# Another beginning for a fused attention, expert and convolution kernel: unit 0 and the tails turned on TensorE, direct rows, new queue orders

## The chip, the cores and the metric

The kernel runs on one core of a Trainium2 chip. The metric is the device time of one execution in microseconds (us). All five engines take part: TensorE (PE) multiplies, VectorE (DVE), ScalarE (ACT) and GpSimd (POOL) work on tiles, and SyncE (SP) issues most of the transfers (DMAs); ACT and POOL issue some.

## The reference

Three layers follow each other; the change is in the first.

```
scores = q @ k.T / sqrt(D)                       # 4 x 8 heads, S = 576, D = 64, float32
cum    = cumsum(maximum(s, 0))
bias   = minimum(-(cum[:, None] - cum[None, :]), 0)
scores = where(causal, -1e9, scores + bias)
attn   = softmax(scores) @ v                     # -> x, [4, 576, 512]
x      = experts(x)      # 8 experts of 512 x 1024 x 512, one per token, relu, times its probability
h      = relu(x @ w_in); out = (h * sigmoid(conv3(h))) @ w_out
```

## The kernel before

float32 factors are kept as two float16 parts, "hi" and "lo", so that TensorE can multiply float16. The 32 heads are cut into 8 units of 4 heads. A unit's 576 rows are 512 main rows and 64 tail rows; the tails of all heads are prepared once.

Preparing unit u: `load` (L158) brings k and q into the buffers `st`; `split_hi` (ACT, L241) and `split_lo` (DVE L247 for units 0 and 1, POOL L249 and L250 after that) make the two parts; `turn` (L259) turns them with a DMA transpose on SP, two per unit, each for one half (e) of the rows; `copy` (DVE, L267) assembles 64 partitions of the tile `K1[u % 3]`. Rows 64 to 69 of that tile hold the running sum of s, in three float16 digits `cp` that `decay` makes for all heads. They go to DRAM (`ex`, `ext`; L593, L594, issued by ACT) and from there into the tile (`extra`, L263). Row 70 holds the row maxima.

Row maxima: `stage_a` (L334) multiplies hi by hi in up to 15 pieces per unit, DVE reduces each (L337); `max_turn` (PE, L400) and `max_out` (ACT, L405) make a row `mr`, which `max_row` (L412, L415) sends into row 70. Then `scores` (L432), exponentials on ACT (L471 to L477), the products with v (L504), normalization, and a store to `xd`. The v parts come by `loadv` (L168, L172; 12 transfers for one call) and `split_v`.

Order: a main loop of steps t. A unit has 14 steps, so unit u begins at step 14u, and step 0 is the first score product of unit 0. The table `PAR` says at which step, before its own beginning, a unit loads ('load', 'loadq' later for q), splits and turns ('at': k, q, turn half 0, turn half 1, extra), copies ('cp'), runs its pieces ('pa' over 'pn' steps) and makes its maxima ('mx'). The table 'start' orders the beginning. Each engine takes its instructions in the order in which the program emits them. SP's and ACT's transfers take eight semaphores in turn, and a transfer waits until the earlier transfer with its semaphore has landed.

The unit's chain at the beginning is: loads, splits, four transposes of unit 0 (halves apart), copies, rows from `ex`, six pieces for heads 0 and 1, `mr`, six pieces for heads 2 and 3, step 0. `turn_tail` (L277) turns the tails with four more transposes.

Of the kernel before, what the change touches and what calls it, by code (L numbers as in the profile page):

```python
# [9 lines left out]
F32 = mybir.dt.float32  # L10
F16 = mybir.dt.float16
# [31 lines left out]
class Keep:  # L43
# [6 lines left out]
PAR = {'u1': {'sv': -6, 'pa': -9, 'pn': 4, 'mx': -3},  # L50
 'u2': {'at': (-24, -23, -20, -20, -19), 'cp': (-18, -16), 'lv': -11, 'sv': -2, 'pa': -14, 'pn': 8, 'mx': -6},
 'u3': {'load': -37, 'loadq': 6, 'at': (-33, -28, -28, -27, -26.9), 'cp': (-23, -21), 'sv': -1, 'pa': -20, 'pn': 14, 'mx': -6},
 'u': {'load': -48,
       'loadq': 8,
       'at': (-38, -34, -28, -31, -26),
# [19 lines left out]
 'start': {'st': -4.88,  # L75
           'lk1': -3.883,
           'c1': -1.883,
           'pa': -1.88,
           'lq1': -0.877,
           'sk1': -0.843,  # L80
           'tt': -0.84,
           'lv0': -0.837,
           'sq1': -0.834,
           'lk2': -0.834,
           'mt0a': 0.129,
           'mo0a': 0.163,
           'mr0a': 0.166,
           'ct': 0.4,
           'pb': 0.377,
           'c2': 1.0,  # L90
           'pt': 1.003,
           'sv0': 1.103,
           'T10': 1.106,
           'mtt': 1.203,
           'mot': 1.3,
           'T11': 2.26,
           'x1': 2.269,
           'mtb': 2.297,
           'mob': 2.34,
           'mrt': 3.091,  # L100
           'lq2': 3.1,
           'mrb': 4.003,
           'z': 5.0,
           'lv1': 5.997},
# [8 lines left out]
def attention(tc, ctx, q, k, v, s, xd, rt, hook):  # L113
# [80 lines left out]
    for n in ("k", "q"):  # L194
        for b in range(B):
            G.dma_start(nt[32 * b:32 * b + 32, AT[n]], src[n][b, :, 512:576].rearrange("h (p t) d -> p h (t d)", t=2))
    constants(G, T1)
    make_identity(nc, ident)
    for t in (triq, trik, tailq):
        G.memset(t, 0.0)  # L200
    for e in range(2):
        r = slice(64 * e, 64 * e + 64)
        G.memset(tailk[r, e], 0.0)
        G.memset(tailk[r, 1 - e], -2.0 ** 15)
    for tq, tk, n in ((triq, trik, 64), (tailq, tailk, 32)):
# [63 lines left out]
    def split_tail(n):  # L269
        i = AT[n]  # L270
        a, h = nt[:, i].rearrange("p h (t d) -> p (h t) d", t=2), ht[:, i]
        A.activation(h[:, :, 1 - i], a, AF.Copy, scale=scale[n])
        V.scalar_tensor_tensor(h[:, :, i], in0=a, scalar=scale[n], in1=h[:, :, 1 - i], op0=ALU.mult, op1=ALU.subtract)

    def turn_tail():
        for b in range(B):
            Q.dma_start_transpose(out=T2[:, b].rearrange("d n (x p) -> d (n x) p", p=32), in_=ht[32 * b:32 * b + 32].rearrange("p n x y d -> p (n x y d)"))  # L277

    def copy_tail():
        for r, i in ((64, 0), (67, 1)):  # L280
            Q.dma_start(T1[r:r + 3, :, i], ext.rearrange("j (b h) c -> j b (h c)", b=B))
        for i in range(2):
            V.tensor_copy(T1[0:64, :, i], T2[64 - 64 * i:128 - 64 * i, :, i])
# [123 lines left out]
    def max_row(u, hs=slice(0, 4), tails=True):  # L407
        n = 0
# [173 lines left out]
    decay(0)  # L582
    split_hi(0, "k")
    split_lo(0, "k")
    decay(1)
    split_hi(0, "q")
    decay(2)
    split_lo(0, "q")
    for i in range(2):
        for e in range(2):  # L590
            turn(0, e, slice(i, i + 1))
    for e in range(2):
        A.dma_start(ex[:, e].rearrange("j r c -> r j c"), cp[:, :, 256 * e:256 * e + 256])  # L593
# [23 lines left out]
    def second_a():  # L617
        for f in P0[6:12]:
            f()()

    begin_tasks = dict(
        lk1=lambda: load(1, "k"), lq1=lambda: load(1, "q"), st=lambda: (split_tail("k"), split_tail("q")), tt=turn_tail, ct=copy_tail,
        lv0=lambda: loadv(0, 0, G), lv1=lambda: loadv(0, 1, G if PAR["h"]["vq"] else Q), c1=lambda: constants(G, K1[1]), c2=lambda: (constants(G, K1[2]), tctx.close()),
        pa=begin_a, sk1=lambda: split_qk(1, "k"), sq1=lambda: split_qk(1, "q"), mt0a=lambda: max_turn(0, first, False), mo0a=lambda: max_out(0, first, False),
        mr0a=lambda: max_row(0, first, False), T10=lambda: turn(1, 0), T11=lambda: turn(1, 1), x1=lambda: extra(1),
        pb=second_a, sv0=lambda: split_v(0), lk2=lambda: load(2, "k"), lq2=lambda: load(2, "q"),
        pt=lambda: [P0[12 + i]()() for i in range(3)], mtt=lambda: max_turn(0, None), mot=lambda: max_out(0, None), mrt=lambda: max_row(0, None),
        mtb=lambda: max_turn(0, second, False), mob=lambda: max_out(0, second, False), mrb=lambda: max_row(0, second, False),
        z=lambda: Q.dma_start(xd[NT:NT + 128].rearrange("p (j c) -> p j c", c=256), bc(zero[:, None, 0:256], [128, 4, 256])))
# [889 lines left out]
```

## Time and profile before

| | us |
|---|---|
| three runs | 718.02, 721.0, 721.49; median 721.0 |
| the profiled execution | 722.48, of which 720.8 from the first to the last instruction |
| attention | 0 to about 250 |
| routing and first experts | about 250 to 300 |
| experts | to about 490, then the third layer to 720.8 |

Over the span PE is busy 639.1 us (89%), DVE 446.1, ACT 385.8 and POOL 251.7. Some of the profile's views give busy time by stretch, with the granted clock of TensorE as a share of 2.4 GHz (0.50 is 1.2 GHz, the lower of its two levels). A timeline row begins with its start and its length; the bracket at its end is the idle time before it and what ended it. Rows with "q" behind the engine (SPq) are issues of transfers.

### The profile page before, as it was taken

The page shows a single profiled execution, that of the slowest core. Times are in us where ns is not written, and L with a number is a line of the kernel's source. Part 1 is how long each engine was busy: PE and PEld are TensorE (multiplying, and loading weights), DVE is VectorE, ACT ScalarE, POOL GpSimd, SP SyncE. Part 2 cuts the span into 40 slices and gives each one's busy share as a digit, 9 for nine tenths or more (in the row PEclk, how much of TensorE's full clock was granted, in tenths as well). Part 3 has the DMA queues.
Part 4 walks back from the last instruction along what each step waited for, and adds up shares of the span by engine and source line. Part 5 has one row for each costly group of instructions (what it writes and reads, how often), then busy time and mean ns, then how long its engine had stood idle before and what let it go on. Part 6 is the DMA issues. An engine that isn't in the chain of part 4 may idle for free. (4 is left out here: it accounts for less than half of the span.)

```text
span 720.8 us, 15276 instructions
## 1 busy us (share of the span) xinstructions
PE 639.1 (89%) x5087; PEld 399.5 (55%) x5087; DVE 446.1 (62%) x852; ACT 385.8 (54%) x650; POOL 251.7 (35%) x362
## 2 busy tenths in 40 slices
PE   0469699999999756899899899999889999999997
PEld 0247578887888633444444344444357766665443
DVE  5765578867976599563695868663129976455000
ACT  4142748785778656553653655532129965546010
POOL 9536766575144039932234544433100000000000
PEclk9985969997999859899999999999999999999999
DMA  9977474874568425899899996964184000000111
GB/s 183 183 148 138 68 163 107 159 138 84 128 206 272 126 69 185 248 335 239 200 311 257 272 280 194 259 128 104 48 149 101 16 15 16 30 30 16 58 45 58
DMA packets 175580, 103.89 MB, mean 144 GB/s; under 512 B 128150, under 2 KB 153534, under 8 KB 175486
## 3 DMA queue, kind: packets, MB, share of 16 engines
q1 hardware_dynamic: 170878, 89.70, 52.7%
q0 software_dynamic: 4272, 12.93, 5.9%
q8 instruction: 46, 0.75, 0.4%
q14 instruction: 48, 0.39, 0.2%
q10 hardware_dynamic: 336, 0.11, 0.1%
HBM read 62.20 MB, written 15.31 MB: 108 GB/s over the span
## 5 line engine op out<-in xcount | busy, mean ns | idle before, releaser
L1129 PE MATMUL hp<-r,xt 128*128 x504 | 114.1, 383 | 10.2 <-ACT xt L1160 7.1
L1129 PE MATMUL yp<-r,ht 128*128 x504 | 112.2, 379 | 1.7 <-PEq L1236 1.7
L1327 PE MATMUL hp<-yt,wi 128*128 128x288 f16 x768 | 97.1, 289 | 2.8 <-DMA yt<-yd 2.8
L1375 PE MATMUL o<-wo,g 128*128 128x512 f16 x432 | 94.5, 379 | 0.0
L1327 PEld LDWEIGHTS <-wi 128*128 128x128 f16 x768 | 75.8, 99 | 24.4 <-DMA yt<-yd 3.3
L1129 PEld LDWEIGHTS <-xt 128*128 128x128 f16 x504 | 49.8, 99 | 71.0 <-ACT xt L1160 9.6
L1129 PEld LDWEIGHTS <-ht 128*128 128x128 f16 x504 | 48.5, 98 | 57.4 <-issue 1.8
L1085 DVE SCALAR_TENSOR_TENSOR r<-st,r 128x512 f32 (+3 forms) x80 | 70.7, 950 | 6.2 <-ACT r L1074 4.5
L1074 ACT ACTIVATE r<-st 128x512 f32 (+3 forms) x84 | 57.1, 762 | 26.7 <-SPq L1122 22.1
L1375 PEld LDWEIGHTS <-g 128*128 128x128 f16 x432 | 42.3, 98 | 49.5
L337 DVE TENSOR_REDUCE mx<-za 128x1 f32<-128x384 f32 (+4 forms) x97 | 56.9, 602 | 17.4 <-PE za L334 16.7
L1190 POOL DMA_INDIRECT yd<-ys,idx x21 | 21.7, 1034 | 126.3 <-DVEq L1113 87.5
L476 ACT ACTIVATE phi<-z,lnes 128x512 f16<-128x512 f32 (+1 forms) x80 | 50.1, 627 | 29.3 <-PE z L435 29.2
L432 PE MATMUL z<-k 71*128 71x256 f16 (+2 forms) x320 | 55.4, 301 | 6.7 <-DMA k<-mr 4.2
L334 PE MATMUL za<-k 70*128 70x256 f16 (+2 forms) x160 | 37.4, 314 | 26.8 <-DMA k<-ex 20.8
L488 DVE TENSOR_TENSOR plo<-z,phi 128x512 f16<-128x512 f32 (+1 forms) x80 | 48.2, 603 | 12.1 <-ACT z L477 11.5
L1344 DVE SCALAR_TENSOR_TENSOR c<-hb,cw,c 128x576 f32<-128x576 f32 x32 | 26.1, 816 | 37.0 <-ACT c L1338 37.0
L504 PE MATMUL o<-v,p 128*128 128x65 f32 x256 | 48.1, 301 | 0.0
L477 ACT ACTIVATE z<-z,lnes 128x512 f32<-128x512 f32 (+1 forms) x80 | 47.9, 598 | 0.0
L1378 ACT ACTIVATE s<-o 128x512 f32<-128x512 f32 x18 | 10.7, 597 | 63.9 <-PE o L1375 63.9
L504 PE MATMUL o<-vv,phi 128*128 128x65 f16 (+1 forms) x512 | 43.7, 207 | 0.0
L504 PEld LDWEIGHTS <-phi 128*128 128x128 f16 x544 | 43.5, 112 | 0.0
(270 smaller groups left out, 1146.2 us busy)
## 6 DMA issues: line engine op xcount, KB each, us to landing
st<-in_moe_w_dram SPq DMA_DIRECT2D x8, 2048.0 KB
st<-in_moe_w_dram SPq DMA_DIRECT2D x24, 512.0 KB
out_dram<-s SPq DMA_DIRECT2D x18, 256.0 KB
st<-in_k_dram SPq DMA_DIRECT2D x16, 256.0 KB
st<-in_q_dram SPq DMA_DIRECT2D x16, 256.0 KB
xd<-xh SPq DMA_DIRECT2D x16, 256.0 KB
k<-in_moe_w_dram SPq DMA_DIRECT2D x8, 512.0 KB
s<-in_moe_w_in_dram SPq DMA_DIRECT2D x16, 256.0 KB
```

The source lines that it names most:

```text
L334: PE.matmul(out, lhsT=l, rhs=r, start=start, stop=stop, skip_group_check=True)
L337: return lambda: V.tensor_reduce(out, z.rearrange("p (e c) -> p e c", e=m), axis=AX.X, op=ALU.max)
L432: PE.matmul(out, lhsT=ks[i], rhs=qs[i], start=first and not i, stop=False, skip_group_check=True)
L476: A.activation(hi[:, 0:n], z[:, 0:n], AF.Exp, bias=lnes, scale=1.0 / SC)
L477: A.activation(p[:, 0:n], z[:, 0:n], AF.Exp, bias=lnes, scale=1.0 / SC)
L488: (V if md == "a" else G).tensor_tensor(lo[:, 0:n], p[:, 0:n], hi[:, 0:n], op=ALU.subtract)
L504: PE.matmul(out, lhsT=w, rhs=x, start=first, stop=last, skip_group_check=True)
L1074: i = self.nc.scalar.activation(hi, src, AF.Copy, scale=self.scale[w])
L1085: i = nc.vector.scalar_tensor_tensor(lo, in0=src, scalar=sc, in1=hi, op0=ALU.mult, op1=ALU.subtract)
L1129: i = self.nc.tensor.matmul(out, lhsT=lhsT, rhs=self.rings[w][:, c, k, bass.ds(s, 1), f], **kw)
L1327: PE.matmul(st[x][:, n, 0:HN], lhsT=wi[:, c, k, m], rhs=t[:, n, a + k], start=k + a + c == 0, stop=k == 3 and a == 4)
L1375: PE.matmul(o, lhsT=g[:, a, k, 128 * i:128 * i + 128], rhs=wo[:, c, k], start=j == 0, stop=j == 23)
```

## The change

- Unit 0 and the tails are turned on TensorE: `turned` multiplies four 128x128 blocks by an identity into a PSUM tile, and ACT or DVE copies it out in float16. Unit 0 has 8 such tiles, the tails 8. The eight DMA transposes at the beginning are gone.
- `extra_first`: unit 0's rows of `cp` go straight from on-chip memory into the tile, in 12 transfers on SP, instead of through `ex`. `ex` and `ext`, for the other units and the tails, are written by POOL.
- The tails are loaded by SP (k's ahead of the rows, q's after unit 1's loads) instead of POOL; the masks are made in another order; unit 0's maxima rows are issued by ACT.
- `busy`: idle products of 512 columns whose result nobody reads: 10 ahead of unit 0's turns, 4 ahead of the pieces, and 1 ahead of each of unit 0's 12 pieces.
- The pieces of heads 2 and 3, which were all emitted ahead of step 0's products, are spread over steps 1 to 4. Unit 1's pieces begin at step 7 instead of 5.
- Later units: q of unit 3 is loaded at step 6 instead of 11; units from 4 on load, split and turn 3 steps sooner, and half 1 is still turned ahead of half 0. q's lo part of unit 1 is made by POOL instead of DVE.

```diff
- 'u': {'load': -48,
+ 'u': {'load': -51,
        'loadq': 8,
-       'at': (-38, -34, -28, -31, -26),
+       'at': (-41, -37, -31, -34, -26),
...
+    def turned(h, i, j, out, copy):
+        z = zps.tile([128, 512], F32, name="z") if j % 2 else ops.tile([128, 512], F32, name="o")
+        for m in range(4):
+            PE.matmul(z[:, 128 * m:128 * m + 128], lhsT=h[:, i, 4 * j + m].rearrange("p y d -> p (y d)"), rhs=id16, start=m == 0, stop=m == 3, skip_group_check=True)
+        z = out(z, j)
+        if copy == "A":
+            A.activation(z[0], z[1], AF.Copy)
+        else:
+            V.tensor_copy(*z)
...
+    def extra_first(j):
+        for r, n in ((64, 0), (67, 1)):
+            for e in range(2):
+                Q.dma_start(K1[0][r + j:r + j + 1, e, n].rearrange("o (h c) -> o h c", h=NH), cp[0:NH, j, 256 * e:256 * e + 256])
...
+    def busy(z, n):
+        for _ in range(n):
+            PE.matmul(z.rearrange("p (x c) -> p x c", c=128), lhsT=id16, rhs=bc(id16[:, None], [128, 4, 128]), start=True, stop=True, skip_group_check=True)
...
     def max_row(u, hs=slice(0, 4), tails=True):
-        n = 0
+        n, Q = 0, nc.sync if u else nc.scalar
...
-    for i in range(2):
-        for e in range(2):
-            turn(0, e, slice(i, i + 1))
-    for e in range(2):
-        A.dma_start(ex[:, e].rearrange("j r c -> r j c"), cp[:, :, 256 * e:256 * e + 256])
...
+    busy(mps.tile([128, 512], F32, name="mt"), 10)
+    for j in range(3):
+        decay(j)
+        extra_first(j)
+        if j:
+            split_hi(0, "kq"[j - 1])
+    for e in range(2):
+        G.dma_start(ex[:, e].rearrange("j r c -> r j c"), cp[:, :, 256 * e:256 * e + 256])
...
+    turn_first("k", "AAVA")
+    copy(0, "k")
+    turn_first("q", "AVAA")
+    copy(0, "q")
+    for n in ("k", "q"):
+        load(1, n)
+    load_tail("q")
...
+        ttk=lambda: turn_tail("k", range(4), "AVAV"), ttq=lambda: turn_tail("q", range(4), "AVAV"),
+        pb=lambda: second_a(range(6, 8)), pc=lambda: second_a(range(8, 10)), pd=lambda: second_a(range(10, 12)),
```

Three places in the engines' order carry the prediction. The first is SP's queue at the beginning, behind unit 0's own loads. Before (`h`, `k_229`: unit 0's parts and their turned tile; `t_142`: the turned tails; `mr`: the maxima row of heads 0 and 1; `k_384`: unit 1's turned tile):

```order
L259 DMA_TRANSPOSE k_229<-h 128x16x64 x4
L263 DMA k_138<-ex 3x2x1024 x2
L158 DMA st_112<-in_k_dram 128x4x128 x2
L158 DMA st_112<-in_q_dram 128x4x128 x2
L277 DMA_TRANSPOSE t_142<-k_144 128x32x32 x4
L158 DMA st_111<-in_k_dram 128x4x128 x2
L412 DMA k_138<-mr 1x4x128 x2
L281 DMA t_141<-ext 3x4x512 x2
L259 DMA_TRANSPOSE k_384<-st_111 128x32x64 x2
```

The same stretch after the change:

```order
L193 DMA k_143<-in_k_dram 32x8x128 x4
L318 DMA k_138<-cp 1x4x256 x12
L165 DMA st_112<-in_k_dram 128x4x128 x2
L165 DMA st_112<-in_q_dram 128x4x128 x2
L193 DMA k_143<-in_q_dram 32x8x128 x4
L322 DMA t_141<-ext 3x4x512 x2
L165 DMA st_111<-in_k_dram 128x4x128 x2
L165 DMA st_112<-in_q_dram 128x4x128 x2
L276 DMA_TRANSPOSE k_391<-st_111 128x16x64 x4
```

The eight transposes and the maxima row left this queue; 16 small transfers came in ahead of unit 1's loads.

The second is the meeting of SP's and ACT's transfers behind unit 1's rows, with the semaphores that each waits for (DMAHW0 to DMAHW7 are the eight). SP, from unit 3's q to v's third transfer:

```order
L165 DMA st_112<-in_q_dram 128x4x128 [waits DMAHW3_49]
L165 DMA st_112<-in_q_dram 128x4x128 [waits DMAHW4_49]
L175 DMA nv<-in_v_dram 64x4x64 [waits DMAHW5_49]
L175 DMA nv<-in_v_dram 64x4x64 [waits DMAHW6_49]
L175 DMA nv<-in_v_dram 64x4x64 [waits DMAHW7_49]
```

ACT, from the maxima row of heads 2 and 3 (emitted in step 5):

```order
L454 ACTIVATE mr<-mt 8x128 [waits DMAHW5_49,PE_49]
L461 DMA k_138<-mr 1x4x128 [waits DMAHW7_49,Activation_49]
L461 DMA k_138<-mr 1x4x128 [waits DMAHW1_49]
L525 ACTIVATE phi<-z,lnes 128x512
L526 ACTIVATE z<-z,lnes 128x512
```

In the program the maxima row takes DMAHW7 ahead of the third v transfer, so that transfer now waits until the row has landed. Behind it on SP stand nine more v transfers, unit 2's two transposes, and unit 1's maxima row.

The third is SP's queue around the maxima row of unit 2 (`k_140<-mr`), which step 28 needs. Before:

```order
L168 DMA nv<-in_v_dram 64x8x64 x8
L172 DMA nvt<-in_v_dram 32x4x64 x4
L158 DMA st_112<-in_k_dram 128x4x128 x2
L412 DMA k_140<-mr 1x8x128 x2
L415 DMA t_141<-mr 1x2x128
L259 DMA_TRANSPOSE k_1271<-h 128x32x64 x2
```

After:

```order
L175 DMA nv<-in_v_dram 64x8x64 x8
L179 DMA nvt<-in_v_dram 32x4x64 x4
L165 DMA st_112<-in_k_dram 128x4x128 x2
L276 DMA_TRANSPOSE k_1275<-h 128x32x64
L461 DMA k_140<-mr 1x8x128 x2
L464 DMA t_141<-mr 1x2x128
L276 DMA_TRANSPOSE k_1275<-h 128x32x64
```

One of unit 4's two transposes now stands ahead of that row. The same is so for units 5, 6 and 7 and the rows of units 3, 4 and 5.

## Rows read from the trace of the kernel before

**Rows 1.** Busy time by stretch: length, each engine, granted clock, DMA share, GB/s.

```profile
0.00:20.00 20.00, 0.00 (x0) 0.00 (x0) 10.21 (x16) 7.64 (x11) 18.80 (x45) 1.00 0.95 180
...
80.00:100.00 20.00, 14.23 (x143) 10.79 (x142) 11.95 (x26) 8.86 (x19) 14.57 (x44) 0.70 0.82 159
...
120.00:140.00 20.00, 19.55 (x305) 16.98 (x303) 17.72 (x52) 16.31 (x31) 14.14 (x19) 1.00 0.64 113
```

**Rows 2.** SP's timeline, 0 to 160 us: start, length, line, transfer, count.

```profile
8.54 7.99 SPq L259 DMA_TRANSPOSE k<-h  x4
16.64 1.68 SPq L263 DMA_DIRECT2D k<-ex  x2
...
22.33 7.94 SPq L277 DMA_TRANSPOSE t<-k  x4
...
32.20 1.35 SPq L412 DMA_DIRECT2D k<-mr  x2
...
50.20 5.34 SPq L168 DMA_DIRECT2D nv<-in_v_dram  x8
55.59 2.01 SPq L172 DMA_DIRECT2D nvt<-in_v_dram  x4
...
79.21 7.13 SPq L259 DMA_TRANSPOSE k<-st  x2
...
97.30 0.99 SPq L158 DMA_DIRECT2D st<-in_k_dram  x2
99.38 1.47 SPq L412 DMA_DIRECT2D k<-mr  x2
```

**Rows 3.** Timeline: first piece, first maxima row, steps 0, 14, 28, 56, 69.

```profile
20.82 0.37 PE L334 MATMUL za<-k 70*128 70x128 f16 x2 [20.82 <-DMA k<-ex]
...
27.43 0.25 ACT L405 ACTIVATE mr<-mt 8x128 f16<-8x128 f32 x1
...
35.28 1.03 PE L432 MATMUL z<-k 71*128 71x512 f16 x2 [3.59 <-DMA k<-mr]
...
74.50 0.59 PE L432 MATMUL z<-k 71*128 71x512 f16 x2 [0.63 <-DMA k<-mr]
...
108.34 0.59 PE L432 MATMUL z<-k 71*128 71x512 f16 x2
...
152.49 0.59 PE L432 MATMUL z<-k 71*128 71x512 f16 x2
...
178.64 0.22 PE L435 MATMUL z<-tailk,identm 128*128 128x128 f16 x1
```

**Rows 4.** Timeline at two pauses of PE: DVE's copies of units 3 and 6.

```profile
89.25 0.69 DVE L267 COPY k<-k 64x2048 f16<-64x2048 f16 x1 [4.00 <-DMA k<-st]
...
90.71 0.32 PE L334 MATMUL za<-t 70*64 70x64 f16 x4 [5.62 <-DVE mx L337]
...
161.04 1.30 DVE L267 COPY k<-k 64x2048 f16<-64x2048 f16 x1 [3.73 <-DMA k<-h]
```

**Rows 5.** Busy time in short stretches, columns as in rows 1.

```profile
60.00:64.00 4.00, 4.00 (x32) 3.30 (x30) 1.76 (x6) 0.60 (x2) 3.83 (x6) 0.50 0.99 144
...
72.00:76.00 4.00, 3.37 (x54) 3.00 (x51) 2.34 (x6) 4.00 (x8) 1.23 (x3) 1.00 0.05 14
```

**Rows 6.** Groups by line and form: count, busy us, mean ns, idle before.

```profile
L488 DVE TENSOR_TENSOR plo<-z,phi 128x512 f16<-128x512 f32 x9 | 6.2, 684 | 3.8 <-ACT z L477 3.7
L337 DVE TENSOR_REDUCE mx<-za 128x1 f32<-128x384 f32 x11 | 5.9, 553 | 0.5 <-PE za L334 0.2
...
L334 PE MATMUL za<-k 70*128 70x512 f16 x8 | 4.7, 596 | 0.4 <-DVE mx L337 0.2
...
L250 POOL TENSOR_TENSOR st<-st,st 128x1024 f16<-128x1024 f32 x2 | 4.2, 2125 | 0.2
...
L247 DVE SCALAR_TENSOR_TENSOR h<-st,h 128x1024 f16<-128x1024 f32 x2 | 2.5, 1248 | 3.5 <-ACT h L241 3.5
...
L856 ACT ACTIVATE xT<-mt 128x512 f16<-128x512 f32 x28 | 16.6, 594 | 0.0
```

More of the change, by code (lines that the diff above doesn't have):

```diff
@@ L44 @@
     pass
[L50 to L53 removed]
+PAR = {'u1': {'sv': -6, 'pa': -7, 'pn': 5, 'mx': -3},
+ 'u2': {'at': (-24, -23, -21, -20.9, -20), 'cp': (-16, -15), 'lv': -11, 'sv': -2, 'pa': -14, 'pn': 8, 'mx': -6},
+ 'u3': {'load': -37, 'loadq': 1, 'at': (-33, -30, -28, -27, -26.9), 'cp': (-21, -20), 'sv': -1, 'pa': -20, 'pn': 14, 'mx': -6},
+ 'u': {'load': -51,
        'loadq': 8,
[L55 removed]
+       'at': (-41, -37, -31, -34, -26),
        'cp': (-25, -22),
@@ L74 @@
        'ps': 18},
[L75 to L104, printed above, removed]
+ 'start': {'lv0': -30,
+           'thk': -29,
+           'hk1': -28,
+           'hq1': -27,
+           'wm': -26,
+           'pa': -25,
+           'mt0a': -24,
+           'mo0a': -23,
+           'mr0a': -22,
+           'thq': -21,
+           'lk1': -20,
+           'tlk': -19,
+           'tlq': -18,
+           'lq1': -17,
+           'xt': -16,
+           'lk2': -15,
+           'lq2': -14,
+           'T1k': -13,
+           'T1q': -12,
+           'x1': -11,
+           'ttk': 0.6,
+           'ttq': 1.0,
+           'pb': 1.1,
+           'ct': 2.0,
+           'pt': 2.1,
+           'sv0': 2.4,
+           'c2': 2.5,
+           'mtt': 3.0,
+           'mot': 3.1,
+           'mrt': 3.2,
+           'pc': 3.3,
+           'pd': 4.0,
+           'mtb': 5.0,
+           'mob': 5.1,
+           'mrb': 5.2,
+           'z': 6.0,
+           'lv1': 6.1},
  'r': {'cut': 12, 'w1': 6, 'w2': 8, 'w3': 22},
@@ L182, in attention, with load_tail @@
         load(0, n)
+    def load_tail(n):
+        for b in range(B):
+            Q.dma_start(nt[32 * b:32 * b + 32, AT[n]], src[n][b, :, 512:576].rearrange("h (p t) d -> p h (t d)", t=2))
+    load_tail("k")
     cp = cum.tile([32, 3, S], F16, name="cp")
@@ L267, in copy, with tail_hi @@
         V.tensor_copy(U[u, 1][0:64, :, i], U[u, 2][64 - 64 * i:128 - 64 * i, :, i])
-    def split_tail(n):
+    def tail_hi(n):
         i = AT[n]
[L271 to L277, printed above, removed]
@@ new lines, in turn_first, with turn_tail @@
+    def turn_first(n, engines):
+        if (0, 2) not in U:
+            U[0, 1], U[0, 2] = K1[0], st2.tile([128, 2, 2, 1024], F16, name="k2")
+        for j, copy in enumerate(engines):
+            turned(U[0, "h"], AT[n], j, lambda z, j: (U[0, 2][:, :, AT[n], 256 * j:256 * j + 256].rearrange("d e (x p) -> d e x p", p=64), z.rearrange("d (x e p) -> d e x p", x=4, e=2)), copy)
+    def turn_tail(n, js, engines):
+        for j, copy in zip(js, engines):
+            turned(ht, AT[n], j, lambda z, j: (T2[:, :, AT[n], 128 * j:128 * j + 128].rearrange("d b (x p) -> d b x p", p=32), z.rearrange("d (x b p) -> d b x p", x=4, b=B)), copy)
@@ L342, in piece @@
             z = aps.tile([128, 512], F32, name="za")
+            if halves:
+                busy(z, 1)
             for x, h in enumerate(hs):
@@ L615, in begin_a, with second_a @@
             f()()
-    def second_a():
-        for f in P0[6:12]:
-            f()()
+    def second_a(r):
+        for i in r:
+            P0[i]()()
     begin_tasks = dict(
[L622 to L627, printed above, removed]
+        lv0=lambda: loadv(0, 0, G), c2=lambda: (constants(G, K1[2]), tctx.close()),
+        thk=lambda: tail_hi("k"), thq=lambda: tail_hi("q"), tlk=lambda: tail_lo("k"), tlq=lambda: tail_lo("q"),
+        hk1=lambda: split_hi(1, "k"), hq1=lambda: split_hi(1, "q"), lk1=lambda: split_lo(1, "k"), lq1=lambda: split_lo(1, "q"),
+        wm=lambda: busy(mps.tile([128, 512], F32, name="mt"), 4),
+        pa=begin_a, mt0a=lambda: max_turn(0, first, False), mo0a=lambda: max_out(0, first, False), mr0a=lambda: max_row(0, first, False),
+        ttk=lambda: turn_tail("k", range(4), "AVAV"), ttq=lambda: turn_tail("q", range(4), "AVAV"),
+        pb=lambda: second_a(range(6, 8)), pc=lambda: second_a(range(8, 10)), pd=lambda: second_a(range(10, 12)),
@@ L628, in attention @@
         mtb=lambda: max_turn(0, second, False), mob=lambda: max_out(0, second, False), mrb=lambda: max_row(0, second, False),
+        xt=extra_tail, ct=copy_tail, lk2=lambda: load(2, "k"), lq2=lambda: load(2, "q"),
+        T1k=lambda: [turn(1, e, slice(0, 1)) for e in range(2)], T1q=lambda: [turn(1, e, slice(1, 2)) for e in range(2)], x1=lambda: extra(1),
+        pt=lambda: second_a(range(12, 15)), mtt=lambda: max_turn(0, None), mot=lambda: max_out(0, None), mrt=lambda: max_row(0, None),
+        sv0=lambda: split_v(0), lv1=lambda: loadv(0, 1),
```

67 lines of the change are left out of this document (35 added, 32 removed).

## The prediction

> **What bounds the kernel now.** I read the busy time by stretch first [rows 1]. TensorE is the busiest engine, but not at the beginning: it does nothing in the first 20 us, 14.23 us of work between 80 and 100 at a mean granted clock of 0.70, and 19.55 of 20 from 120 on at 1.00. So the attention's later part is bound by TensorE, and its first 100 us by what TensorE waits for. The timeline then says what that is [rows 3]: the first piece waited until 20.82 for unit 0's rows from DRAM, and step 0 until 35.28 for the first maxima row, which ACT had written at 27.68 (27.43 + 0.25). SP's timeline shows why [rows 2]: the rows were sent at 16.64, right behind the four transposes of unit 0 (8.54 to 16.53), and the maxima row at 32.20, behind the tails' transposes (22.33 to 30.27). Two transposes hold SP for 7.13 us. The queue is the bound of the beginning.
>
> The steps' times carry the rest [rows 3]: step 14 at 74.50, 28 at 108.34, 56 at 152.49, step 69's end at 178.64. Two undisturbed units between 28 and 56 take 44.15, so 22.1 a unit and 1.58 a step. Unit 1 took 33.8, or 11.8 more, and steps 56 to 69 took 26.1, or 5.6 more than 13 steps of 1.58. Both have a pause in them [rows 4]: DVE stands in its copy of unit 3 for 4.00 us because the transposes are late, TensorE then pauses 5.62; with unit 6's copy it is 3.73. Behind a pause TensorE works at the lower of its levels.
>
> The granted clock reads 1.00 even in the first 20 us, in which TensorE does nothing [rows 1]. But a lone 512-column product takes 596 ns on average in the first 80 us [rows 6], and the pair that opens a step takes 1.03 us at step 0 against 0.59 at step 14 [rows 3]. So I take TensorE to be at the lower level from its first product until shortly before 72, where the column turns from 0.50 to 1.00 behind some 10 us of nearly full work [rows 5].
>
> **The change, part by part.**
>
> *To step 0.* SP loses the transposes. It gains 4 tail loads and 12 direct rows; neither is in the trace of before, the nearest row is v's 0.67 us a transfer (5.34 / 8) [rows 2], so 10.7 for 16. They begin behind the loads of s, k and q (about 3.3 us, from two pairs at 0.99 and a start of 1.3) and end at 14.0. A landing takes 1.7: the maxima row's issue ended at 33.55, step 0 began at 35.28 [rows 2, 3]. The rows are there at 15.7. At 0.5 us a transfer it is 13, at 0.9 it is 19. Unit 0's tiles come about as soon: k's parts are done at 8.54, where its transpose starts [rows 2]; q's follow some 2.3 us later (an ACT split, and DVE's 1.25 [rows 6]); then six copies on ACT at 0.59, with two copies and two assemblies on DVE at 0.69 beside them [rows 4, 6], end near 14.5. I take 15.7 for the first piece, 5.1 earlier.
>
> From there to the maxima row took 6.6 (20.82 to 27.43) [rows 3]. Each of the six idle products costs between nothing (TensorE waits there for DVE's reductions anyway) and 0.596 [rows 6]; the first two run while the rows are awaited, so 0 to 2.4, and I take 1.0, nearer to nothing because of those waits. The row is written at 23.5, ACT issues it at once (1.35), it lands 1.7 later: step 0 at 26.6, **8.7 earlier**.
>
> For that last move the Trainium skill has a rule that speaks against it. "DMA: Bandwidth & Descriptors", section "Issuing engines are not separate DMA queues", says that using several engines to issue saves only the issuing sequencer's time, which is usually small beside the transfer. By the rule step 0 would keep the 4.5 us between 27.68 and 32.20; the rows put those 4.5 us in SP's queue, in front of the issue, so my sum counts them as saved. No row of before shows a maxima row issued by ACT.
>
> *To step 14.* Here work comes back. Six pieces and the tails' turns now come after step 0, and unit 1's maxima wait for unit 0's second row. DVE, between its sixth reduction (23) and its twelfth, has five subtractions of parts (four at 1.25 and a small one, 5.3), six copies (4.1), six reductions (3.6), three for the tails (2.1) and one lo part (0.7), from [rows 4, 6]: 15.8 us. It waits for TensorE as well, which at the lower level is nearly full; nothing to 8 us, and I take 4. That gives 43; transposition and copy of the maxima, about 0.9, and row and landing, 3.05, give 47. At the second place in the order, SP's third v transfer waits for this landing. Behind it: ten v transfers (6 x 0.67 + 2.01 = 6.0), two transposes (7.13), the row from `ex` (1.68), unit 1's maxima row (1.47) and its landing (1.7) [rows 2]: step 14 at 65.0, **9.5 earlier**. Unit 1's own turns hide: they wait on SP for the first maxima row's landing (26) and take about 7, so they are in place by 36, and DVE copies them only near 40.
>
> *To step 28.* SP again: unit 4's q (0.99), unit 3's transposes (7.13), `ex` (1.68), twelve v transfers (7.35), a load (0.99), one transpose of unit 4 (3.6), unit 2's maxima row (1.47), a landing (1.7): 24.9 from 63.3, so 88.2 [rows 2]. The engines need 22.1 from 65.0, so 87.1. I take 88.5, **19.8 earlier**. The pause of unit 3 goes, because its transposes end at 72 and the copies come at step 21, near 76. What is late next is the row itself, by about a microsecond.
>
> *To step 56 and 69.* Two units at 22.1 give 132.7. At the third place the v transfers (step 48) now have a transpose behind them before unit 4's row: 7.35 + 3.6 + 1.47 + 1.7 = 14.1 against 8 steps of 1.58, 12.6. Step 56 waits 1.5: 134.2, **18.3 earlier**. Then 20.5 instead of 26.1 if unit 6's pause is gone (its turns start three steps, 4.7 us, sooner; it waited 3.73), or 26.1 if the wait at 56 costs the clock again. I take half: **21.1 earlier** at step 69. Later stretches have no such pauses, the expert weights' loads are tied to steps, and the following layers move along.
>
> **The sum** is 722.48 - 21.1 = 701.4 for the profiled execution, which lies 1.5 above the median of 721.0, so 699.9. All five landings were taken at 1.7, from a row with no 256 KB load just ahead of it. I add 3 us for that: **703**.
>
> **Rivals.**
>
> *The upper level comes early.* The idle products are 512 columns wide and run where TensorE stood idle. If the level rises with them and holds, DVE's 4 us of waiting go: step 14 at 61, step 28 at 84.5, 56 at 130.2 and 69 at 150.7, so 27.9 earlier, and 693. For it: ten products of 0.4 to 0.6 us in a row. Against it: before, nearly 10 us of full work stood ahead of the rise [rows 5], and after the tenth product TensorE has gaps again. The Trainium skill's "TensorE: Matmul & The Clock Gate", section "Part 1: The HAM clock gate (the "warmup" mystery)", says that the throttled state is the default and that activity releases it, which is on this rival's side.
>
> *A row issued by ACT comes no sooner,* because it is held up in landing, not in the queue: the chain starts 4.5 us later, 707.5. This is what the Trainium skill's rule on issuing engines, above, would make of it.
>
> *The sooner loads and turns are not sooner,* since SP is so full that it reaches them when it did before. Unit 3's pause with its slow stretch stays: the 10.3 us between steps 14 and 28 are lost again, 713. For it: SP's chain to step 28 has 1 us of slack at most.
>
> *Slower: the maxima row behind the transpose.* For units 2 to 5 a transpose of a later unit stands ahead of the row. It can start only when POOL has made q's lo part (2.13 [rows 6], behind its scaling and ACT's split), three steps (4.7 us) after the split is emitted. If POOL is late, the row is late, and TensorE stops at the unit's beginning. A pause of 5.62 cost 11.8 in all before. Two such stops of the four eat the gain (703 + 23.6 = 727); with one it is 715. The deciding point is a row about 5 us behind its step. Against it: the transpose's half (3.6), the row and its landing (3.2) fit into the five steps (7.9) between them if POOL is on time.
>
> **How the numbers follow.** Chances: the forecast 0.46 (its own range 697 to 711), early clock 0.16, no gain from ACT's queue 0.10, nothing sooner 0.14, rows behind transposes 0.08 at 727 (a single stop lies within the range), and 0.06 for what I haven't seen, on both sides. 690 holds the early clock's 693 with 3 us to spare; 716 holds the one in which nothing comes sooner. About 0.5% (3.6 us) is what a measurement of this kernel can tell from no change. All cases but the last named lie below 717.4; with a part of the nothing-sooner case and of the unseen counted as no change: faster 0.86, same 0.06, slower 0.08.
>
> **What would show it.** The first piece near 15.7, released by a row from `cp`; step 0 near 26.6; DVE without long idle time between steps 0 and 7; unit 2's transposes on SP near 53, right behind v; step 14 near 65 with TensorE released by the maxima row; no copy of unit 3 or 6 waiting on a transpose; short waits of steps 28 and 56 for `mr`. I am wrong if step 0 is later than 31 (the direct rows are slow), if unit 2's transposes start after 60 (the meeting of the two queues costs more), or if steps 28, 42 or 56 wait 5 us for their rows.

## The result, and the profile of the changed kernel

711.64 us median (709.87 to 714.46, four runs) against 721.25 for the kernel before beside it (718.02 to 722.09): ratio 0.9882, 95% interval 0.9842 to 0.9922. That is 9.6 us faster, inside the predicted range of 690 to 716, but about half of the 18 us forecast. The profiled execution took 709.87 us, its span 708.2. In this section and the next, runs more than 1.5% above the fastest of the same kernel, a slower state of the chip, are left out of medians and ratios.

The timeline of the changed kernel, at the places of [rows 2, 3] (in the new numbering L381 is a piece, L449 turns the maxima, L454 writes a maxima row, L481 opens a step, L484 closes step 13 or 69):

```profile
5.99 7.81 SPq L318 DMA_DIRECT2D k<-cp  x12
...
14.30 0.28 PE L381 MATMUL za<-k 70*128 70x128 f16 x2 [0.61 <-DVE k L284]
...
21.52 0.25 ACT L454 ACTIVATE mr<-mt 8x128 f16<-8x128 f32 x1
21.80 1.79 ACTq L461 DMA_DIRECT2D k<-mr  x2
...
28.20 1.04 PE L481 MATMUL z<-k 71*128 71x512 f16 x2 [5.74 <-DMA k<-mr]
...
47.98 1.03 PE L481 MATMUL z<-k 71*128 71x512 f16 x2 [2.99 <-DMA k<-mr]
...
48.91 0.63 PE L381 MATMUL za<-k 70*128 70x128 f16 x4
...
56.03 6.62 SPq L276 DMA_TRANSPOSE k<-h  x2
63.10 1.65 SPq L280 DMA_DIRECT2D k<-ex  x2
...
69.89 0.40 PE L449 MATMUL mt<-ident,mx 128*18 128x128 f32 x2 [1.37 <-DVE mx L412]
...
70.61 1.40 SPq L461 DMA_DIRECT2D k<-mr  x2
...
70.85 0.30 PE L484 MATMUL z<-tailk,identm 128*128 128x128 f16 x1
...
73.77 1.04 PE L481 MATMUL z<-k 71*128 71x512 f16 x2
...
101.81 0.59 PE L481 MATMUL z<-k 71*128 71x512 f16 x2
...
152.01 0.59 PE L481 MATMUL z<-k 71*128 71x512 f16 x2
...
171.85 0.22 PE L484 MATMUL z<-tailk,identm 128*128 128x128 f16 x1
```

The steps stand beside those of before like this:

| | before | predicted | changed | difference |
|---|---|---|---|---|
| step 0 | 35.28 | 26.6 | 28.20 | -7.1 |
| step 14 | 74.50 | 65.0 | 73.77 | -0.7 |
| step 28 | 108.34 | 88.5 | 101.81 | -6.5 |
| step 56 | 152.49 | 134.2 | 152.01 | -0.5 |
| step 69's end | 178.64 | 157.5 | 171.85 | -6.8 |

Read the last column down. Seven microseconds are won at the beginning and are gone at step 14; 5.8 are won between 14 and 28, lost between 28 and 56, and 6.3 are won again up to step 69. From there on the difference keeps up to the end of the attention: its last step comes 6.8 sooner (232.17 against 238.96). That is a third of the 21.1 us forecast for step 69. Behind the attention the profiled execution was another 5.8 us shorter than the one before; further down stands why this is chance as far as the runs show.

Busy time by stretch, columns as in [rows 1], from 24 to 80 us:

```profile
24.00:28.00 4.00, 0.00 (x0) 0.00 (x0) 2.30 (x2) 2.03 (x3) 3.50 (x4) 0.50 1.00 211
...
44.00:48.00 4.00, 1.01 (x22) 0.70 (x21) 2.63 (x4) 2.45 (x5) 3.86 (x8) 0.87 0.56 159
48.00:52.00 4.00, 3.86 (x24) 2.77 (x25) 2.81 (x5) 2.35 (x5) 0.00 (x0) 0.50 0.98 244
...
56.00:60.00 4.00, 3.89 (x28) 2.74 (x26) 1.60 (x5) 1.24 (x2) 3.83 (x3) 0.50 0.74 112
...
72.00:76.00 4.00, 3.26 (x30) 2.43 (x28) 3.32 (x3) 4.00 (x10) 3.84 (x6) 0.50 0.46 132
76.00:80.00 4.00, 4.00 (x30) 3.34 (x28) 3.20 (x9) 1.74 (x3) 3.92 (x6) 0.50 0.96 130
```

TensorE waits for the first maxima row (24 to 28) and for the second (44 to 48). Behind the second wait it is nearly full, at the lower level: 3.86 and 3.89 of 4 at 0.50. It is not SP that decides here: SP has sent unit 1's rows from `ex` by 64.75 and then waits for the maxima row, which TensorE turns only at 69.89 and SP sends at 70.61. TensorE reaches step 14 without a wait; from 70.9 to 73.8 it multiplies by v.

And the later stretch in which the second gain is lost:

```profile
132.00:136.00 4.00, 3.33 (x46) 2.60 (x46) 3.86 (x11) 2.98 (x6) 3.20 (x2) 1.00 0.76 181
136.00:140.00 4.00, 2.55 (x32) 1.62 (x31) 3.94 (x10) 1.02 (x4) 1.97 (x7) 0.89 0.72 162
140.00:144.00 4.00, 4.00 (x30) 3.38 (x29) 1.83 (x4) 2.33 (x5) 3.79 (x4) 0.50 0.90 130
```

DVE is full (3.86, 3.94), TensorE pauses behind it (2.55), then works at 0.50.

### The profile page after: what moved, and what is told of

Read it like the earlier page. It is cut to its first block, busy times and chain, and to the rows that moved or that the text cites. A ratio compares the mean times of both kernels' runs of the same rounds, so it can differ in the third digit from the quotient of the medians.

```text
span 708.2 us, 15490 instructions
## 1 busy us (share of the span) xinstructions
PE 644.5 (91%) x5177; PEld 403.8 (57%) x5177; DVE 451.3 (64%) x858; ACT 390.4 (55%) x660; POOL 253.1 (36%) x358
## 5 line engine op out<-in xcount | busy, mean ns | idle before, releaser
L1386 PE MATMUL hp<-yt,wi 128*128 128x288 f16 x768 | 95.6, 286 | 2.6 <-DMA yt<-yd 2.6
L1386 PEld LDWEIGHTS <-wi 128*128 128x128 f16 x768 | 75.1, 98 | 23.5 <-DMA yt<-yd 2.8
L384 DVE TENSOR_REDUCE mx<-za 128x1 f32<-128x384 f32 (+4 forms) x97 | 57.4, 603 | 18.7 <-PE za L381 18.2
L1249 POOL DMA_INDIRECT yd<-ys,idx x21 | 23.9, 1136 | 122.6 <-DVEq L1172 77.7
L481 PE MATMUL z<-k 71*128 71x256 f16 (+2 forms) x320 | 54.8, 298 | 12.1 <-DMA k<-mr 8.7
L1247 ACT ACTIVATE ys<-yp,pp 128x512 f16<-128x512 f32 x21 | 14.3, 683 | 53.6 <-PE yp L1188 35.7
```

What stands on the lines that cost most here:

```text
L384: return lambda: V.tensor_reduce(out, z.rearrange("p (e c) -> p e c", e=m), axis=AX.X, op=ALU.max)
L481: PE.matmul(out, lhsT=ks[i], rhs=qs[i], start=first and not i, stop=False, skip_group_check=True)
L1386: PE.matmul(st[x][:, n, 0:HN], lhsT=wi[:, c, k, m], rhs=t[:, n, a + k], start=k + a + c == 0, stop=k == 3 and a == 4)
```

## The experiments

Each is timed against the kernel before on the same chip; ratios carry 95% intervals. One profile gives the times of the steps. "Attention's end" is the start of its last step's last product: 238.96 before, 232.17 in the changed kernel.

**Which half gives the gain: e_begin and e_later.**

```diff
# e_begin: the changed kernel with the tables 'u2', 'u3', 'u' of before
# e_later: the kernel before with the new tables 'u2', 'u3', 'u'
```

> The new beginning with the tables of before for units 2 and later (unit 1's stays new). If the gain comes from the later units' sooner loads and turns alone: step 14 stays near 74, unit 3's pause at its copy comes back, step 28 is near 108, and the whole is 719 to 722. Rival (the beginning's 7 us at step 0 carry through whatever the tables are): step 28 near 101, the whole about 712.

> The beginning of before with the new tables for units 2 and later. If the gain comes from the later units' tables alone: step 0 at 35.3 and step 14 near 74.5 as before, no pause of some 5 us in unit 3's copy, step 28 near 102, and the whole 711 to 714. Rival (the tables can only be met when SP is free as early as in the new beginning): the pause stays, step 28 near 108, and the whole 719 to 722.

e_begin: 721.11 us, ratio 0.9983 (0.9948 to 1.0019). Step 0 at 31.66, step 13's end at 74.7, unit 3's pause and unit 6's are back (its copies wait 1.94 and 3.87), attention's end 240.0. e_later: 711.78 us, ratio 0.9869 (0.9824 to 0.9915). Step 0 at 35.84 and step 14 at 75.42, as before; no copy of unit 3 or 6 waits, step 28 at 102.94, attention's end 231.6. So the tables of the later units give all of the gain, and the whole new beginning (TensorE's turns, direct rows, idle products, queues) gives nothing that can be measured in the whole's time. My rival, that the tables need SP as free as the new beginning leaves it, falls too.

**Is it the clock: e_noidle, e_fill, e_hold.**

```diff
# e_noidle: without the 10 + 4 + 12 idle products
# e_fill: idle products added at the pauses
+ 'f0': 0.7 (20 of them), 'f7': 7.0 (12), 'f14': 14.0 (8)
# e_hold: e_fill, and 4 more ahead of each step from 0 to 13
```

> The changed kernel without all 26 idle products. Clock theory: the products up to the first maxima row run at the lower level, so that row is written some 2 us later than 21.5; the pauses behind it drop the level anyway, so steps 0 to 14 take the same 45.6 us, and the whole is 0 to 3 us longer, 712 to 715. Rival (the idle products cost more than they give): the row is written at 20 to 21.5, and the whole is 709 to 711.

> 40 more idle products of 512 columns: 20 ahead of step 0, 12 ahead of step 7, 8 ahead of step 14, each time behind the last work that TensorE has before it waits for a maxima row. Clock theory (the pauses at 22.5 to 28.2, 44.8 to 48.0 and 71.0 to 73.8 us drop TensorE to the lower level, and what follows them runs slowly): step 0 stays within 1 us of 28.2, the pair that opens step 0 takes about 0.6 instead of 1.04 us, steps 7 to 13 take about 15 instead of 22.9 us, step 14 comes near 63 instead of 73.8, and the whole takes about 702. Rival (DVE's reductions and copies and the order of the pieces set the time to step 14, the clock only goes along with it): step 14 within 2 us of 73.8, the whole 711 or up to 4 more.

> The kernel with 40 idle products, and 4 more of 512 columns ahead of every step from 0 to 13 (56; 96 in all on top of the changed kernel's 26). In the run with 40, TensorE rose to 1.00 between 28 and 36 us and fell back to 0.50 at 40 and from 52 to 68, and step 13 ended at 71.6. Clock theory (from step 7 to 13 TensorE is bound by its own work at the lower level; kept busy enough it holds the upper one): granted clock above 0.9 from 28 to 70 us, steps 7 to 13 in about 16 instead of 22 us, step 13's end near 64, the whole near 704. Rival (the waits for rows, reductions and copies still pause it, the level falls, and the fill costs 0.43 us a product): clock still near 0.5 to 0.6 from 50 to 70, step 13's end at 80 or later, the whole 718 or more.

e_noidle: 716.92 us, 0.9960 (0.9918 to 1.0002); the first row is written at 23.3, but with the idle products it was written anywhere from 21.5 (changed kernel) to 24.6 (e_begin), step 13 ends at 72.8, 2 us later than in the changed kernel, and attention's end is 232.7 against 232.2. Nearly all of its longer time lies behind the attention (below), so what the 26 products are worth in the whole stays open. e_fill: 709.22 us, 0.9801 (0.9733 to 0.9868); TensorE rose to 1.00 from 28 to 36, steps 0 to 6 took 14.8 instead of 16.6, then the level fell again, 0.50 from 52 to 68, and step 13 ended at 71.6. The rival forecast such a step 13, but step 14 came at 76.5, later than either had it. As the level was not held over steps 7 to 13, the run leaves open whether it bounds them.

e_hold: 718.51 us, 0.9968 (0.9924 to 1.0012). Now the level held from 44 on. Its stretches, and the timeline of step 7 (L498), one group of fill (L384) and step 13's end (L501):

```profile
52.00:56.00 4.00, 3.49 (x28) 2.06 (x27) 1.14 (x3) 1.55 (x2) 0.00 (x0) 1.00 0.55 121
56.00:60.00 4.00, 3.58 (x45) 2.92 (x43) 2.64 (x6) 1.31 (x3) 2.52 (x3) 1.00 0.51 84
60.00:64.00 4.00, 3.63 (x33) 2.13 (x31) 2.34 (x6) 1.24 (x2) 3.83 (x6) 1.00 1.01 145
```

```profile
50.09 3.83 PE L384 MATMUL mt<-id 128*128 128x512 f16 x16
53.75 0.60 PE L498 MATMUL z<-k 71*128 71x512 f16 x2
55.97 1.02 PE L384 MATMUL mt<-id 128*128 128x512 f16 x4
...
74.72 0.22 PE L501 MATMUL z<-tailk,identm 128*128 128x128 f16 x1
```

From step 7's start to the last product of step 13 it took 20.97 us, of which six groups of fill are 24 products at 3.83 / 16, so 5.7: by this estimate the kernel's own work and waits took about 15, against 22.9 (47.98 to 70.85) in the changed kernel. Both theories were half right. The lower level does bound steps 7 to 13; but holding the upper one cost as many microseconds as it gave, and step 7 itself came later (53.75). The attention's end came at 234.1, 1.9 later than in the changed kernel; the rest of the longer time lies behind it.

**Is it where the work stands: e_u1early.**

```diff
- 'u1': {'sv': -6, 'pa': -7, 'pn': 5, 'mx': -3}   copies {5: k, 6: q}
+ 'u1': {'sv': -6, 'pa': -9, 'pn': 4, 'mx': -4}   copies {3: k, 4: q}
```

> Unit 1's 14 pieces from step 5 on (4 steps' worth, as before the change) instead of from step 7 on, its copies at steps 3 and 4, its maxima and row one step sooner. Theory of the order (the 14 pieces behind the pause at step 7 are what makes steps 7 to 13 long): steps 0 to 6 get some 4 us longer and cover their waits, steps 7 to 13 take 17 instead of 22.9, step 14 does not wait for its row, step 13's end near 69 and step 14 near 69 instead of 73.8, the whole 707. Rival (TensorE's work is the same at the same level, wherever it stands): step 13's end within 1.5 us of 70.9, and only the 2.4 us of waiting at step 14 may go; the whole 709 to 712.

709.51 us, 0.9885 (0.9832 to 0.9939). Step 6's end 47.9 (3.1 later), step 13's end 64.8 (6.1 sooner), attention's end 227.1 (5.1 sooner). The kernel before, where unit 1's pieces began at 49.21 and step 7 at 54.49, and e_u1early beside it:

```profile
49.21 0.58 PE L334 MATMUL za<-k 70*128 70x128 f16 x4 [2.44 <-DVE k L267]
...
54.49 1.06 PE L432 MATMUL z<-k 71*128 71x512 f16 x2
...
72.15 0.22 PE L435 MATMUL z<-tailk,identm 128*128 128x128 f16 x1
```

```profile
45.51 0.40 PE L381 MATMUL za<-k 70*128 70x128 f16 x4 [0.30 <-DVE k L284]
...
49.94 0.60 PE L481 MATMUL z<-k 71*128 71x512 f16 x2
...
64.79 0.22 PE L484 MATMUL z<-tailk,identm 128*128 128x128 f16 x1
```

Steps 7 to 13 take 17.7 us before, 22.9 in the changed kernel, in which all of the pieces stand behind step 7, and 14.9 here. TensorE's own work is the same as in the changed kernel; with part of it put into the wait ahead of step 7, it is done at 64.8. From step 0 on it was busy for 31.96 of 36.20 us at a mean granted clock of 0.69, against 35.53 of 42.65 at 0.62: it waits less, and the same work goes faster. The theory of the order holds for the beginning. In the whole's time it doesn't show: this ratio and the changed kernel's are alike.

**The first row's way: e_rowfree and e_rowsp.**

```diff
# e_rowfree: unit 2's loads at 1.9 and 3.25 instead of -15 and -14
# e_rowsp, in max_row:
- n, Q = 0, nc.sync if u else nc.scalar
+ n, Q = 0, nc.sync
```

> Unit 2's loads of k and q behind the tails' copies (step 1.9) and behind unit 0's second tail row (3.25) instead of right behind the tails' rows. If these 1 MB of loads hold up the landing of unit 0's first maxima row: from the end of its issue on ACT to step 0 it takes 2 to 3 us instead of 4.6, and step 0 comes about 2 us sooner. Rival (v's loads on POOL's queue and the rest suffice to hold it up): 4 us or more. Either way step 13's end moves by less than 2 us, since TensorE's work behind it sets that.

> Unit 0's maxima rows issued by SP, as before the change, at the same places in the order. If ACT's queue gives the gain at step 0: SP is held and step 0 comes 3 to 4.5 us later after the row is written. Rival (the gain came from taking the transposes out of SP's queue; SP is free when the row is written): issue within 0.4 us of the writing, and 6 to 7 us from the writing to step 0, as with ACT; instead SP's later transfers, the tails' rows and unit 1's transposes, begin 2 to 4 us later.

e_rowfree (one run, 710.73 us): from the end of the issue (23.83) to step 0 (27.89) 4.06 us, so the row lands late without unit 2's loads too. That they are harmless this does not show: with them gone, SP sent unit 1's transposes at 21.50, into the same place (28.22 in the changed kernel). e_rowsp (one run, 713.14 us), its timeline:

```profile
22.65 0.25 ACT L454 ACTIVATE mr<-mt 8x128 f16<-8x128 f32 x1
22.93 1.20 SPq L461 DMA_DIRECT2D k<-mr  x2
24.24 1.54 SPq L322 DMA_DIRECT2D t<-ext  x2
...
25.89 1.04 PE L481 MATMUL z<-k 71*128 71x512 f16 x2 [2.18 <-DMA k<-mr]
```

SP was free, issued the row at once and ahead of the tails' rows, and it landed 1.76 us after its issue (24.13 to 25.89), not 4.61 (23.59 to 28.20): step 0 came 2.3 us sooner than with ACT, where I had expected it later or at the same distance from the writing. The other profiles bear it out: without idle products ahead of step 0 the row landed 1.73 to 1.85 us after its issue by SP (four profiles: before, e_later, e_rowsp, e_best1) and 4.06 to 5.42 after its issue by ACT (eight). Step 13's end moved by 0.7 (70.2). SP's transposes began at 28.27, no later than at 28.22.

**The later stretch: e_oldu and e_port.**

```diff
# e_oldu: the changed kernel with 'u' of before ('load': -48, 'at': (-38, -34, -28, -31, -26))
# e_port:
- 'at': (-41, -37, -31, -34, -26)
+ 'at': (-39, -37, -31, -34, -26)
```

> The changed kernel with the table of before for units 4 and later alone. In the changed kernel the routing's subtraction on DVE took 2.11 instead of 0.20 us at 128.01, exactly while POOL subtracted unit 6's lo part (127.95 to 130.07), DVE was full from 124 to 140, TensorE paused and ran at 0.50 to 0.76 from 140 to 148. Theory (the sooner splits put POOL's work on that place): the subtraction takes 0.20, steps 49 to 55 take about 11 instead of 15.4 us, but unit 6's copy waits about 3.7 us for its transposes again and steps 63 to 69 take about 14.8 instead of 10.9; the attention's last step within 1.5 us of 232.2, the whole 709 to 713. Rival (DVE is full there from unit 4's and 5's own work, wherever POOL's stands): steps 49 to 55 still take 14 us or more, the attention's last step near 236, the whole near 715.

> The changed kernel with the split of k for units 4 and later at 39 instead of 41 steps ahead, nothing else. Theory (POOL's subtraction of unit 6's lo part holds the routing's subtraction on DVE, 2.11 instead of 0.20 us, and DVE, full from 124 to 140, brings TensorE's pause and its slow stretch at steps 49 to 55): the routing's subtraction takes 0.20 to 1 us, TensorE's clock stays above 0.9 from 136 to 148, steps 49 to 55 take 11 to 12.5 instead of 15.4 us, the attention's last step near 229 instead of 232.2, the whole 707 to 710. Rival (DVE is full from its own work there; two microseconds don't decide): the subtraction is short, but steps 49 to 55 still take 14 us or more; the whole 710 to 713.

In the changed kernel DVE's subtraction for the routing, 0.20 us elsewhere, takes 2.11, and the copy of unit 5 takes 1.10 instead of the 0.69 of [rows 4]; each ends when an instruction of POOL does, or one copy's own time later:

```profile
127.95 2.12 POOL L267 TENSOR_TENSOR h<-st,h 128x1024 f16<-128x1024 f32 x1
128.01 2.11 DVE L976 TENSOR_TENSOR d<-lgs,mf 128x40 f32<-128x40 f32 x1
...
136.53 1.16 POOL L612 TENSOR_TENSOR xh<-x,xh 128x512 f16<-128x512 f32 x1 [1.24 <-ACT xh L611]
137.32 1.10 DVE L284 COPY k<-k 64x2048 f16<-64x2048 f16 x1
```

e_oldu: two runs, 722.23 and 712.34 us, too far apart for a verdict on the whole. The subtraction takes 0.20, the copies of units 4 and 5 take 0.69 and 0.68, and steps 49 to 55 take 10.9 us instead of 15.4; but unit 6's pause is back (3.88 ahead of its copy, steps 63 to 69 13.1 instead of 10.9), and the attention ends at 237.7. Of these 5.5 us, 3.0 arise behind step 69, in a stretch that takes 60.3 us in all the other profiles; why is open. e_port: 714.17 us, 0.9913 (0.9881 to 0.9945), attention's end 235.1. Its timeline:

```profile
131.05 0.20 DVE L976 TENSOR_TENSOR d<-lgs,mf 128x40 f32<-128x40 f32 x1
...
132.71 2.14 POOL L267 TENSOR_TENSOR h<-st,h 128x1024 f16<-128x1024 f32 x1
133.86 1.53 DVE L284 COPY k<-k 64x2048 f16<-64x2048 f16 x1
...
138.89 1.16 POOL L612 TENSOR_TENSOR xh<-x,xh 128x512 f16<-128x512 f32 x1 [0.37 <-ACT xh L611]
139.41 1.37 DVE L284 COPY k<-k 64x2048 f16<-64x2048 f16 x1
```

The subtraction is short, and the slow stretch stayed: steps 49 to 55 took 15.8. My narrow theory, that this one instruction decides, falls. The waiting had only moved: the four copies of units 4 and 5 took 0.85, 2.02, 1.53 and 1.37, 3.0 more than four of 0.69, where the changed kernel lost 1.6 in them and 1.9 in the subtraction.

All the profiles together say more. With the old table for units 4 and later (the kernel before, e_begin, e_oldu) steps 49 to 55 take 10.9 us each time, with a new one (13 profiles) 12.4 to 15.8. The shortest is e_rowfree, whose edit touches only the beginning:

```profile
127.53 2.12 POOL L267 TENSOR_TENSOR h<-st,h 128x1024 f16<-128x1024 f32 x1
127.59 2.12 DVE L976 TENSOR_TENSOR d<-lgs,mf 128x40 f32<-128x40 f32 x1
...
136.91 1.10 DVE L284 COPY k<-k 64x2048 f16<-64x2048 f16 x1
```

```profile
136.00:140.00 4.00, 2.48 (x33) 1.65 (x32) 3.94 (x11) 1.24 (x5) 2.40 (x7) 1.00 0.61 137
140.00:144.00 4.00, 4.00 (x58) 3.63 (x56) 3.53 (x7) 3.68 (x7) 3.71 (x5) 1.00 0.92 135
```

DVE meets POOL there as in the changed kernel (2.12, copies of 0.92, 1.31, 1.07 and 1.10), and TensorE pauses as long (2.48 of 4 busy against 2.55), but the granted clock stays at 1.00, and the steps take 12.4. So of the 4.4 us that the changed kernel loses here, 1.5 come with the meetings and 2.9 with the lower level behind the pause, which the same pause brought in one profile and not in the other.

**Joined: e_best1 to e_best4.** e_best1 is e_u1early with e_rowsp and e_rowfree; e_best2 adds a light fill (10 ahead of step 0, 6 ahead of 7 and of 14, one ahead of each step from 7 to 13); e_best3 is e_u1early with e_port; e_best4 is e_best2 with e_port.

> Three edits on the changed kernel together: unit 1's pieces from step 5 with its copies at steps 3 and 4 and its row a step sooner, unit 0's maxima rows on SP, unit 2's loads at steps 1.9 and 3.25. Theory of the order (TensorE's own work at the lower level between step 0 and step 14 bounds the beginning; what fills its pauses there with unit 1's pieces is a gain): step 0 near 26, step 6's end near 45.5, step 13's end near 62.5 (after: 70.9), the attention's last step near 224.5 (after: 232.2), the whole 703 to 707. Rival (the three gains are the same microseconds, or are given back at unit 1's copies and SP's queue): step 13's end at 64.8 or later as with the sooner pieces alone, the whole 708 to 711.

> The same with a light fill: 10 idle products of 512 columns ahead of step 0, 6 ahead of step 7, 6 ahead of step 14, one ahead of each step from 7 to 13. With 96 products the level held at 1.00 from 44 to 72 us, but step 13 ended at 74.7, as the products took the time that the level gave. If a light fill holds the level too: steps 7 to 13 take 13 us instead of 17, step 13's end near 59, the whole 700 to 704. If it doesn't hold it: step 13's end 1 to 3 us later than without the fill, the whole 1 to 3 us longer.

> The same together with unit 1's sooner pieces, copies and row (which ended the attention's last step at 227.1, with steps 49 to 55 at 14.0 us). If both hold: step 13's end near 65, steps 49 to 55 in 11 to 12.5 us, the attention's last step near 224.5, the whole 704 to 707. If what follows the attention takes its own time whenever it begins (203 to 211 us in the routed experts' stage of the runs so far): the attention ends 7 to 8 us sooner than in the changed kernel, the whole 709 to 712.

> The kernel with the light fill, unit 0's rows on SP, unit 2's later loads and unit 1's sooner pieces (attention's last step at 232.4, after a wait of 1.97 us for a row and a slow stretch at 98 to 111), with the split of k at 39 steps ahead. Theory: steps 49 to 55 in 11 to 12.5 us instead of 15.4, the attention's last step near 229, the whole 708 to 711; if the slow stretch at 98 to 111 was chance, 226 and 704 to 707. Rival: no change, 232 and 711 to 714.

| | us | ratio | step 13's end | attention's end |
|---|---|---|---|---|
| e_best1 | 713.3 | 0.9879 (0.9823 to 0.9936) | 64.8 | 227.7 |
| e_best2 | 713.35 | 0.9879 (0.9812 to 0.9945) | 63.6 | 232.4 |
| e_best3 | 712.92 | 0.9892 (0.9839 to 0.9946) | 64.4 | 230.1 |
| e_best4 | 708.17 | 0.9816 (0.9737 to 0.9896) | 61.1 | 225.8 |

The light fill did hold the level: from step 7 to step 13's last product e_best2 took 12.7 us (50.91 to 63.6) at 1.00 from 52 on, e_best1 15.6 (49.22 to 64.8). What is won comes back as other pauses: unit 2's copy then waits for its transposes (3.86 us in e_best1, 5.86 in e_best4), step 28 of e_best2 for its row (1.97), each with a slow stretch behind it. In the whole's time e_best1, e_best2 and e_best3 missed what I expected of them; e_best4 lies in its range. Steps 49 to 55 took 12.7 us in e_best3 and 14.3 in e_best4, the same split at 39 with which e_port took 15.8. All four are faster than the kernel before; none of them, and not e_fill either, can be told from the changed kernel, whose interval theirs overlap.

## Why the prediction was right in direction and wrong in size

- **To step 0** (-8.7 forecast, -7.1 measured) came out near, but by errors that partly cancel. The 16 transfers of tails and rows ended at 13.80 (14.0 forecast), the first piece came at 14.30 (15.7), released by DVE's copy, not by a row; the first maxima row was written at 21.8 (23.5): 1.7 us sooner than forecast. The row's landing then took 4.6 us and not 1.7. I had put the gain down to ACT's queue; e_rowsp shows that it comes from taking the transposes out of SP's, and that the row sent by ACT at this place lands later. The Trainium skill's "DMA: Bandwidth & Descriptors", section "Issuing engines are not separate DMA queues", says that issuing on several engines saves only the issuing sequencer's time. e_rowsp agrees as far as that goes: SP was free at 22.93, so ACT had no issue time to save; that the row came 2.3 us later by ACT is the trace's, not the section's. The 3 us that I added for landings rest on a misreading: the row whose 1.7 us I took did have two 256 KB loads just ahead of it on SP, as the order listed before the prediction shows too (row at 32.20, ahead of it `30.32 1.78 SPq L158 DMA_DIRECT2D st<-in_k_dram  x2`).
- **To step 14** (-9.5 forecast, -0.7 measured) is the step that failed. Up to step 7 the sum was right (47 forecast, 47.98). From there I let SP's chain of 18 us set step 14 and took TensorE's work as covered; that the change moves the start of unit 1's pieces from step 5 to step 7 I put at nothing. TensorE's work was the bound: 22.9 us for seven steps and unit 1's 14 pieces at the lower level, 5.2 more than before. SP was not late; unit 2's transposes went out at 56.03 (53 forecast), and SP stood ready for unit 1's row from 64.75 to 70.61. From step 0 to step 13's last product TensorE was busy for 35.53 of 42.65 us, and for 30.48 of 36.87 before: what stands behind step 0 now and did not before (six pieces, four of the tails' turns, six idle products) shows as 5.05 us of the 5.8 lost there. That the level and the order bound this stretch is shown by e_hold and e_u1early; that an even sooner step 0 helps little by e_rowsp (2.3 sooner there, 0.7 at step 13).
- **To step 28**: 28.0 us for unit 1 instead of 23.5, but 5.8 less than the 33.8 of before. Unit 3's pause went, as forecast; the lower level stayed until about 80. The row was not late.
- **To step 56** (45.7 us forecast from 28, 50.2 measured): no row was late here either. The loss is steps 49 to 55, where DVE, full, waits for POOL, whose splits the new table puts there. e_oldu shows that the table brings it; e_port that the subtraction alone does not decide; e_rowfree that 2.9 of the 4.4 us are the lower level behind the pause.
- **To step 69**: 19.8 us, better than my 23.3; unit 6's pause is gone, as e_oldu shows by its return. From step 28 to step 69 the two cancel: 70.0 us against 70.3 before.
- **Rivals.** The early clock (693) came true for some microseconds at a time and fell back in each wait for a row. A row that comes no sooner by ACT (707.5) came true in its landing, but the row was written and sent so much sooner that step 0 was won all the same. Rows behind the transposes (727) did not occur: steps 28, 42 and 56 didn't wait. That nothing would be sooner (713) is close in number, but not in mechanism: the sooner tables did act, and the beginning did not.

**Behind the attention** I let the following layers move along; that did not hold either. The routed experts, from the first product into `yp` to the start of the last, took 203.4 to 211.3 us in the 16 profiles, in no order with the edits (203.4 in e_later, 211.3 in e_noidle, 209.1 in e_u1early). In four of them (the changed kernel, e_rowfree, e_u1early, e_best4) the last product into `yp` starts at 499.8, though the attention ends anywhere from 225.8 to 232.2: what was won in the attention was not passed on. What sets that time was not tried. So differences of 5 us at the attention's end are hidden in a median of a few runs, and of the 9.6 us measured only 6.8 are accounted for by the attention; that the whole came to half of the forecast, and not to a third, is luck as far as the runs show.

## What to carry to other kernels

Before work moved off a queue is counted as time won, add up what the next engine must do until the next fixed point, at the level at which it runs there: here 5 us of moved products took back most of 7. A pause costs more than its length when the engine works at its lower level behind it; useful work put into the pause (e_u1early) paid 5.1 us at the attention's end, idle products paid for themselves at best. Change the schedule of the distant units and the beginning apart: here the tables of offsets were worth all of the gain, and a wholly new beginning nothing that the whole shows.

## What the hardware showed beyond that

- DVE and POOL hold each other up. The Trainium skill's "SBUF — State Buffer", section "Who interferes with whom", says that a DVE instruction with two inputs in SBUF, or one in a two-port mode, which a copy can enter, contends with POOL for a shared pair of ports, and that the first to issue keeps the pair for its whole instruction while the other blocks. The trace agrees: the subtraction, with two inputs in SBUF, began 0.06 us behind POOL's and took 2.11 us instead of 0.20, ending 0.05 behind it; copies of 0.69 took 0.85 to 2.02. Whether those copies run in such a mode no run shows.
- The same transfer of a row landed 1.76 us after its issue by SP and 4.61 after one by ACT with SP's transfers ahead of it; which of these delayed it was not tried further. ACT's queue alone is not it: unit 0's second main row, sent by ACT too, ended its issue at 45.77 in the changed kernel and released step 7 at 47.98, 2.21 later.
- Idle products raised the granted clock: in e_fill, with TensorE full of them, it read 0.57 from 24 to 28 and 1.00 from 28 to 32, where the changed kernel read 0.50 in both. In the changed kernel it read 0.87 from 44 to 48, TensorE waited from 45.0 to 48.0, and from 48 to 52 it read 0.50.
